# Start addresses of TensorE's operand tiles moved to multiples of 256 bytes

## The chip, the cores and the metric

The kernel runs on one core of a Trainium2 chip. The metric is device time in microseconds (us), from the start to the end of one execution; the median of 3 timed executions of the kernel before is 1410.64 us (1410.63 to 1410.92). TensorE does the matrix products, VectorE (DVE), ScalarE (ACT) and GpSimd (POOL) the elementwise work, and DMA queues move data between the device memory and SBUF, the on-chip memory of 128 partitions. A tile lies at the same byte address in each partition, and this case is about that address.

## The reference

Three layers follow each other. Everything is float32.

```python
# 1. retention: q, k, v of (8 batches, 8 heads, 576 positions, 64)
scores = q @ k.T / sqrt(64)
x = (scores * gamma[h] ** (i - j) where i >= j else 0) @ v     # -> 4608 tokens x 512
# 2. mixture of 8 experts, each token goes to one
logits = x @ w_gate + modality_bias[modality_id]
e = argmax(logits);  gate = softmax(logits)[e]
x = gate * (relu(x @ w1[e]) @ w2[e])                           # 512 -> 1024 -> 512
# 3. MLP
h = x @ w_in                                                   # 512 -> 2048
out = (h - tanh(h)) @ w_out                                    # 2048 -> 512
```

## The kernel before

**Stages.** The program runs three stages, one after the other, with a few steps of overlap. The attention stage goes through 36 tiles of 128 tokens in plain float32 (L309, L345, L353, L368) and routes the tokens (L409 to L461). The experts' stage goes through 12 units of 400 tokens of one expert, and the MLP stage through 9 blocks of 512 tokens.

**Matrix products.** In the last two stages each operand is split into a high and a low part of type float32r, so that a product takes three matmuls: high by high, high by low, low by high. A step (one of the 8 slices of 128 hidden features of an expert, or of the 16 of the MLP) has 12 matmuls for the first product (`blocks`, L657: 4 pieces `k` of the contraction by three) and 12 for the second (L859 to L861 in the experts' stage, L934 to L936 in the MLP stage). The second product of a step comes 2 (experts) or 3 (MLP) steps after the first.

**What streams and what is held.** In every first product (L657) the tokens stream: `xh[:, k]` and `xl[:, k]`, 400 columns of 4 bytes per partition in the experts' stage, and `yh[:, k]`, `yl[:, k]`, 512 columns, in the MLP stage; 128 x 128 pieces of weight are held. In the experts' second product `hi` and `lo` (400 columns) stream. In the MLP's second product the weights `wout` (512 columns) stream and pieces of `hi` and `lo` are held.

**Where tiles lie.** Memory comes from a stack of pools at each end of SBUF; a tile takes the address that the sizes of the tiles below it leave. Tiles of even units come from pool `xT_p[0]` and those of odd units from `xT_p[1]` (L136). The MLP's blocks alternate in the same way between `P["yT"]` and a pool `yTb` (L892). The scratch tiles `eh` and `el` of the MLP stage are cut from `xT_p[0]` (L896), which is free then.

**What sets the order.** Engines run their instructions in the order in which the code issues them (`manual_schedule`); a semaphore wait is added where a tile or its memory is reused. In the MLP stage `post3` gives ACT and DVE their work for a step, and `prep3` loads and splits the next block's tokens.

Of the kernel before, what the change touches and what calls it, by code (L numbers as in the profile page):

```python
# [8 lines left out]
F32 = mybir.dt.float32  # L9
F32R = mybir.dt.float32r  # L10
# [9 lines left out]
B, H, S, D = 8, 8, 576, 64  # L20
# [6 lines left out]
PERIOD = 9  # L27
# [4 lines left out]
NRG = NTILE // RG  # L32
UE = 400
SE = -(-UE // 128)
UMIN = -(-NT // UE)
UMAX = (NT - E) // UE + E
CAP = NT
# [2 lines left out]
UB = 512  # L40
# [3 lines left out]
KD = DM // 128  # L44
# [56 lines left out]
def kernel(tc, A, out):  # L101
    nc = tc.nc
    with ExitStack() as ctx:
# [14 lines left out]
        xT_p = [pool("xTa", 1), None]  # L118
        idt0 = keep.tile([128, SE], I32, name="idt0")
        pick = keep.tile([1, 2], I32, name="pick")  # L120
# [10 lines left out]
        xT, P = {}, {}  # L131

        def turn_rows(u, s, src, tp):

            if s == 0:
                p = xT_p[u != "t" and u % 2]  # L136
                xT[u] = (p.tile([128, KD, UE], F32R, name="xh"), p.tile([128, KD, UE], F32R, name="xl"))
            xh, xl = xT[u]
            w = min(128, UE - s * 128)
            c = slice(s * 128, s * 128 + w)  # L140
            tp = tp[:, :, 0:w]
            for k in range(KD):
                nc.tensor.transpose(tp[:, k], src[0:w, k * 128:(k + 1) * 128], ident[0:w, 0:w])
            nc.scalar.copy(out=xh[:, :, c], in_=tp)
            nc.vector.tensor_tensor(out=xl[:, :, c], in0=tp, in1=xh[:, :, c].bitcast(F32), op=ALU.subtract)  # L145

        def load_ids(base, idt):
            with nc.allow_non_contiguous_dma(reason="one id per partition and tile"):
                nc.sync.dma_start(out=idt, in_=slot_d[bass.ds(base, SE * 128), 0:1].rearrange("(s p) o -> p (s o)", p=128))

# [48 lines left out]
        with tc.manual_schedule():  # L199
            c1, c1r = ExitStack(), ExitStack()  # L200
            p1, p1r = pools(c1), pools(c1r)
            att = p1("att", 1)
# [10 lines left out]

            mask = att.tile([128, 2, TL], F32, name="mask")
            gx = att.tile([128, PERIOD, H // 2, TL], F32, name="gx")
            vsc = att.tile([128, PERIOD, H], F32, name="vsc")
            step = att.tile([128, PERIOD, H // 2], F32, name="step")
            state = [att.tile([128, H // 2, D], F32, name=f"state{i}") for i in range(2)]
            wg = const.tile([128, KD, 32], F32, name="wg")
            ltri = const.tile([128, 128], BF16, name="ltri")  # L220
            ones = const.tile([128, 128], BF16, name="ones")
# [296 lines left out]
            for t in range(NTILE):  # L518
                g, r = divmod(t, RG)
# [31 lines left out]
                if t == (EARLY + 1) * RG + 1:  # L551
# [3 lines left out]
                    load_ids(base, idt0)  # L555
                    x0 = [gld.tile([128, 2, DM], F32, name="vk") for _ in range(SE // 2)]
                    x0 = [x0[s // 2][:, s % 2] for s in range(SE)]
                    for s in range(SE):
                        gather_rows(s, idt0, x0[s], EARLY * RG * TL)
# [7 lines left out]
            def early(s):  # L567
                turn_rows(0, s, x0[s], ps_sc.tile([128, KD, TL], F32, name="sc") if s < 3 else ps_x.tile([128, 2, KD, TL], F32, name="xp")[:, 0])
# [63 lines left out]
            ls_last = route_a(g)  # L632
            for s in range(2, SE):
                early(s)
# [38 lines left out]
            yT = {}  # L673
# [5 lines left out]

            def split_y(b, yr, k, p):  # L680
                if k == 0:
                    yT[b] = (p.tile([128, KD, UB], F32R, name="yh"), p.tile([128, KD, UB], F32R, name="yl"))
                yh, yl = yT[b]
                nc.scalar.copy(out=yh[:, k], in_=yr[:, k])
                nc.gpsimd.tensor_tensor(out=yl[:, k], in0=yr[:, k], in1=yh[:, k].bitcast(F32), op=ALU.subtract)
# [7 lines left out]
            with ExitStack() as c2:  # L693
# [3 lines left out]
                ht_p = p2("ht2", 3)  # L697
# [3 lines left out]
                raws, raw_of, wsp, xg, regs, yos = {}, {}, {}, {}, {}, {}  # L701
                steps = [(u, f) for u in range(UMIN) for f in range(F1)]
                limits = {0: E * CAP, 1: E - 1, 2: NT, 3: 1}
# [47 lines left out]
                def post(i, hp, ht):  # L751
                    if hp is None:
                        split_w(i - 1, 1)
                        return
                    hi = ht_p.tile([128, UE], F32R, name="hi")
                    lo = ht_p.tile([128, UE], F32R, name="lo")
                    nc.scalar.activation(out=hi, in_=hp, func=ACTF.Relu)  # L757
                    nc.vector.scalar_tensor_tensor(out=lo, in0=hp, scalar=0.0, in1=hi.bitcast(F32), op0=ALU.max, op1=ALU.subtract)
                    ht[i] = (hi, lo)
                    if i > 0:  # L760
                        split_w(i - 1, 1)
                        load_raw(i - 1 + F1)
                        raws.pop(i - 1)
                    split_w(i + 2, 0)
                    if steps[i] in ((0, 0), (0, 1)):
                        for f in range(3 * i + 3, min(F1, 3 * i + 6)):
                            load_raw(f)
# [7 lines left out]
                yr0 = [None]  # L775
                idts = {}

                def swap():

                    c1r.close()  # L780
                    po, pr = pools(ctx), pools(c2)
                    P["yT"], P["yr"], P["wo"] = (po(n, 1, side="right") for n in ("yT", "yr", "wo"))
                    P["acc"] = po("acc", 4, space=PSUM, side="right")
                    P["id"] = pr("id2", 2, side="right")
                    P["yo"] = pr("yo2", 1, side="right")
                    cv2 = pr("cv2", 1, side="right")
                    cvs2.extend(conv(cv2, A["wo"][f], dst=wo_d[f]) for f in range(F3))
                    cvs2.extend(conv(cv2, A["wi"][f], winh[:, f], winl[:, f]) for f in range(F3))
                    for f in range(len(cvs2)):
                        fill2.extend(cvs2[f][1])  # L790
                        if f > 0:
                            fill2[-3] = lambda a=fill2[-3], b=cvs2[f - 1][2]: (a(), b())
                        if f + 2 < len(cvs2):
                            fill2[-1] = lambda a=fill2[-1], b=cvs2[f + 2][0]: (a(), b())
                    fill2.reverse()

                def prep(u, f):
                    if u == "t":
                        return
                    if u == 0 and f == 0:  # L800
                        rest_a()
                    if u == 0 and f == 1:
                        rest_b()
                    if u == 0 and f == 2:
                        rest_c()
                        swap()
                    d = 2 if u == 0 else 0
                    if u + 1 < UMIN:
                        if f == d:
                            idts[u + 1] = ids_of(u + 1)  # L810
                        if f == d + 1:
                            gather(u + 1, idts.pop(u + 1))
                        for s in {6: (0, 1), 7: (2, 3)}.get(f, ()) if u == 0 else range(f - F1 + SE + 1, f - F1 + SE + 2):
                            if 0 <= s < SE:
                                tr_x(u + 1, s)
                    while pend and cvs2:
                        load_raw(pend.pop(0))
                    if f == 3 and u - 1 in yos:
                        store(u - 1)
                        if (u - E + 1) * UE + E - 1 >= UB and yr0[0] is None:  # L820
                            yr0[0] = load_y(0)
                    if u == UMIN - 1 and f == 4:
                        load_wout(0, P["wo"])
                    if u == UMIN - 1 and f >= 4:
                        split_y(0, yr0[0], f - 4, P["yT"])
                    if u == 0 and f in (3, 4):
                        cvs2[f - 3][0]()
                    for _ in range(2 - f % 2 if u > 0 or f > 4 else 0):
                        if fill2:
                            fill2.pop()()  # L830

                def finish(u, acc):
# [6 lines left out]
                    yos[u] = yo  # L839
                    if u == "t" or u == UMIN - 1:  # L840
                        store(u)
# [32 lines left out]

                run_units(range(UMIN), None)
                while fill2:
# [10 lines left out]
            with ExitStack() as c3:  # L887
                p3 = pools(c3)
                wo_p = p3("wo3", 1)
                for f in range(1, F3):  # L890
                    load_wout(f, wo_p)
                yT2 = [P["yT"], p3("yTb", 1)]  # L892
                ht_p3 = p3("ht3", 4)
                o_p = p3("o", 1)
                vs = {}
                eh, el = (xT_p[0].tile([128, 3, UB], F32, name=n) for n in ("xh", "xl"))  # L896

                def post3(i, hp, ht):
                    old = vs.pop(i - 1, None)
# [89 lines left out]
```

## Time and profile before

| | us |
|---|---|
| median of the timed executions | 1410.64 |
| the profiled execution | 1411.06 |
| its span, first to last instruction | 1409.3 |
| attention stage, to the first matmul of the experts | 153 |
| experts' stage, to the first matmul of the MLP | 450 |
| MLP stage, to the end | 806 |

The stages overlap by a few steps; their borders are the starts of the first matmuls at L657, 152.99 and 603.40 us after the start. A row of the timeline or of the chain of waits begins with its start and its length, both in us, then the engine and the line; `x12` means that 12 instructions stand in the row. Matmuls are pipelined: the length of one row with one matmul says little, and the distance between the starts of two says what one costs.

### The profile page before, as it was taken

The page shows a single profiled execution, that of the slowest core. Times are in us where ns is not written, and L with a number is a line of the kernel's source. Part 1 is how long each engine was busy: PE and PEld are TensorE (multiplying, and loading weights), DVE is VectorE, ACT ScalarE, POOL GpSimd, SP SyncE. Part 2 cuts the span into 40 slices and gives each one's busy share as a digit, 9 for nine tenths or more (in the row PEclk, how much of TensorE's full clock was granted, in tenths as well). Part 3 has the DMA queues.
Part 4 walks back from the last instruction along what each step waited for, and adds up shares of the span by engine and source line. Part 5 has one row for each costly group of instructions (what it writes and reads, how often), then busy time and mean ns, then how long its engine had stood idle before and what let it go on. Part 6 is the DMA issues. An engine that isn't in the chain of part 4 may idle for free.

```text
span 1409.3 us, 22537 instructions
## 1 busy us (share of the span) xinstructions
PE 1386.3 (98%) x8427; PEld 1206.3 (86%) x8427; DVE 1045.1 (74%) x1762; ACT 692.8 (49%) x1302; POOL 218.2 (15%) x290
## 2 busy tenths in 40 slices
PE   8999999999999999999999999999999999999996
PEld 7888899999999999978888888888888888888884
DVE  5666778888888888568778777787777877778773
ACT  3323444444444444456555555555555555555542
POOL 4555311110000111101101111011110111101101
PEclk9999999999999999999999999999999999999998
DMA  9997644554844446261100001000010000100000
GB/s 372 405 337 261 206 137 130 123 127 142 229 92 92 92 122 169 67 248 32 40 22 30 30 1 42 19 30 30 1 45 16 30 30 0 46 16 1 30 0 30
DMA packets 65266, 136.50 MB, mean 97 GB/s; under 512 B 22656, under 2 KB 29376, under 8 KB 65152
## 3 DMA queue, kind: packets, MB, share of 16 engines
q1 hardware_dynamic: 50368, 96.77, 22.8%
q0 software_dynamic: 7296, 19.57, 4.1%
q10 hardware_dynamic: 7488, 18.67, 3.5%
q8 instruction: 68, 1.11, 0.3%
q14 instruction: 46, 0.38, 0.1%
HBM read 132.95 MB, written 39.80 MB: 123 GB/s over the span
## 4 chain that ended last, share of the span: by engine, by line
PE 51%; issue 5%; POOL 0%; POOLq 0%; ACT 0%
PE hp L657 26%; PE acc L935 8%; PE acc L934 8%; PE acc L936 8%; POOL out_dram L959 0%; POOLq L985 0%; POOL nopt L958 0%; ACT o L956 0%; POOLq L959 0%
## 5 line engine op out<-in xcount | busy, mean ns | idle before, releaser
L907 ACT ACTIVATE xh<-hp 128x512 f32<-128x512 f32 x144 | 86.1, 598 | 313.8 <-PE hp L657 292.1
L657 PE MATMUL hp<-yh,winh 128*128 128x512 f32 x576 | 226.6, 393 | 1.4 <-PEq L880 1.4
L657 PE MATMUL hp<-yl,winh 128*128 128x512 f32 x576 | 226.5, 393 | 0.0
L657 PE MATMUL hp<-yh,winl 128*128 128x512 f32 x576 | 226.4, 393 | 0.0
L935 PE MATMUL acc<-wout,hi 128*128 128x512 f32 x576 | 225.5, 391 | 0.0
L934 PE MATMUL acc<-wout,hi 128*128 128x512 f32 x576 | 225.3, 391 | 0.0
L936 PE MATMUL acc<-wout,lo 128*128 128x512 f32 x576 | 224.7, 390 | 0.0
L909 DVE TENSOR_TENSOR xl<-xh,hp 128x512 f32<-128x512 f32 x144 | 99.1, 688 | 161.2 <-ACT xh L908 161.2
L918 DVE SCALAR_TENSOR_TENSOR xl<-xh,xl 128x512 f32<-128x512 f32 x144 | 128.5, 893 | 15.4 <-DVE xl L917 0.5
L859 PE MATMUL acc<-hi,wh 128*128 128x400 f32 x384 | 137.1, 357 | 0.1
L657 PE MATMUL hp<-xl,wh 128*128 128x400 f32 x384 | 132.8, 346 | 0.5 <-DVE xl L145 0.5
L861 PE MATMUL acc<-hi,wl 128*128 128x400 f32 x384 | 132.7, 346 | 0.0
L657 PE MATMUL hp<-xh,wl 128*128 128x400 f32 x384 | 132.6, 345 | 0.2 <-DVE wl L733 0.2
L657 PE MATMUL hp<-xh,wh 128*128 128x400 f32 x384 | 132.1, 344 | 0.4 <-ACT wh L732 0.4
L860 PE MATMUL acc<-lo,wh 128*128 128x400 f32 x384 | 131.7, 343 | 0.0
L657 PEld LDWEIGHTS hp<-yh,winh 128*128 128x128 f32 x576 | 108.3, 188 | 25.7 <-PEq L880 1.7
L657 PEld LDWEIGHTS hp<-yh,winl 128*128 128x128 f32 x576 | 108.2, 188 | 24.6
L757 ACT ACTIVATE hi<-hp 128x400 fp32r<-128x400 f32 x96 | 48.4, 505 | 163.8 <-PE hp L657 163.8
L934 PEld LDWEIGHTS acc<-wout,hi 128*128 128x128 f32 x576 | 108.2, 188 | 24.2 <-ACT hi L912 0.3
L657 PEld LDWEIGHTS hp<-yl,winh 128*128 128x128 f32 x576 | 108.3, 188 | 23.9
L936 PEld LDWEIGHTS acc<-wout,lo 128*128 128x128 f32 x576 | 108.3, 188 | 23.6 <-DVE lo L913 0.4
L935 PEld LDWEIGHTS acc<-wout,hi 128*128 128x128 f32 x576 | 108.2, 188 | 23.1
(166 smaller groups left out, 2520.0 us busy)
## 6 DMA issues: line engine op xcount, KB each, us to landing
raw<-in_w_dram SPq DMA_DIRECT2D x91, 512.0 KB
qk<-in_qk_dram SPq DMA_DIRECT2D x36, 512.0 KB
vk<-in_vk_dram SPq DMA_DIRECT2D x36, 512.0 KB
y_d<-yo SPq DMA_DIRECT2D x12, 800.0 KB
yr<-y_d SPq DMA_DIRECT2D x9, 1024.0 KB
raw<-in_wo_dram SPq DMA_DIRECT2D x16, 512.0 KB
wo_d<-cv_em ACTq DMA_DIRECT2D x16, 512.0 KB
raw<-in_wi_dram SPq DMA_DIRECT2D x16, 512.0 KB
```

Source lines behind the costliest of these rows:

```text
L657: nc.tensor.matmul(out=hp, lhsT=lhs, rhs=rhs, start=j == 0, stop=j == 3 * KD - 1)
L757: nc.scalar.activation(out=hi, in_=hp, func=ACTF.Relu)
L859: nc.tensor.matmul(out=o, lhsT=wh[:, cs], rhs=hi, start=first, stop=False)
L860: nc.tensor.matmul(out=o, lhsT=wh[:, cs], rhs=lo, start=False, stop=False)
L861: nc.tensor.matmul(out=o, lhsT=wl[:, cs], rhs=hi, start=False, stop=last)
L907: nc.scalar.activation(out=u, in_=hp, func=ACTF.Square)
L909: nc.vector.tensor_tensor(out=v, in0=u, in1=hp, op=ALU.mult)
L918: nc.vector.scalar_tensor_tensor(out=v, in0=s, scalar=SQ_C, in1=v, op0=ALU.add, op1=ALU.mult)
L934: nc.tensor.matmul(out=acc[s], lhsT=hi, rhs=wh, start=first, stop=False)
L935: nc.tensor.matmul(out=acc[s], lhsT=hi, rhs=wl, start=False, stop=False)
L936: nc.tensor.matmul(out=acc[s], lhsT=lo, rhs=wh, start=False, stop=last)
```

## The change

Three things change. The attention stage's constants `vsc` and `step` move into one tile `small` behind `state`, padded to 512 bytes, so that `qk`, `vk`, `vs`, `a` and `state` begin at multiples of 256. The experts' streamed tiles get wider rows: 448 columns allocated for 400 used in `hi`, `lo` and in the odd units' `xh`, `xl`; 512 for 400 in the even units'. The MLP's even blocks take the even units' buffer instead of a pool of their own, a filler of 224 bytes stands ahead of `wout0`, and the scratch tiles, `o` and the MLP's `hi` and `lo` move to other memory. The leftover unit `"t"`, which these inputs don't reach, takes the odd units' buffer.

The start of each streamed or held operand, modulo 256 bytes, as the two programs were built (the matmuls counted are those of one execution):

```
operand                           matmuls      before                     after
qk, vk, vs, a, state (attention)  all of them  192 + 256 n, 192 + 512 n   0
xg (turned by TensorE)            held         128                        0
xh, xl, even units, k = 0 1 2 3   L657: 576    0 64 128 192               0
xh, xl, odd units,  k = 0 1 2 3   L657: 576    128 192 0 64               0
hi, lo of the experts (by turns)  L859-861     0 64 128, 192 0 64         0
weights of the experts            held         0                          0
yh, yl, even blocks (5 of 9)      L657: 960    224                        0
yh, yl, odd blocks (4 of 9)       L657: 768    0                          0
wout0 (one step in 16)            L934-936:108 224                        0
wout1 to wout15                   1620         0                          0
winh, winl, hi, lo of the MLP     held         0                          0
ident (streams through transposes)             128                        128
```

The 400 columns of the experts' stage are 1600 bytes, 512 columns are 2048, and 128 columns 512.

```diff
+LINE = 256
+UL = -(-UE * 4 // LINE) * LINE // 4
+PAD = 224
...
-                p = xT_p[u != "t" and u % 2]
-                xT[u] = (p.tile([128, KD, UE], F32R, name="xh"), p.tile([128, KD, UE], F32R, name="xl"))
+                p = xT_p[1 if u == "t" else u % 2]
+                xT[u] = [p.tile([128, KD, UB if p is xT_p[0] else UL], F32R, name=n)[:, :, 0:UE] for n in ("xh", "xl")]
...
-            vsc = att.tile([128, PERIOD, H], F32, name="vsc")
-            step = att.tile([128, PERIOD, H // 2], F32, name="step")
             state = [att.tile([128, H // 2, D], F32, name=f"state{i}") for i in range(2)]
+            small = att.tile([128, -(-PERIOD * H * 6 // LINE) * LINE // 4], F32, name="small")
+            vsc = small[:, 0:PERIOD * H].rearrange("p (r h) -> p r h", h=H)
+            step = small[:, PERIOD * H:PERIOD * H * 3 // 2].rearrange("p (r h) -> p r h", h=H // 2)
...
-                    yT[b] = (p.tile([128, KD, UB], F32R, name="yh"), p.tile([128, KD, UB], F32R, name="yl"))
+                    yT[b] = [p.tile([128, KD, UB], F32R, name=n) for n in ("xh", "xl")]
...
-                    hi = ht_p.tile([128, UE], F32R, name="hi")
-                    lo = ht_p.tile([128, UE], F32R, name="lo")
+                    hi, lo = (ht_p.tile([128, UL], F32R, name=n)[:, 0:UE] for n in ("hi", "lo"))
...
-                    P["yT"], P["yr"], P["wo"] = (po(n, 1, side="right") for n in ("yT", "yr", "wo"))
+                    po("line", 1, side="right").tile([128, PAD // 4], F32, name="line")
+                    P["yr"], P["wo"] = (po(n, 1, side="right") for n in ("yr", "wo"))
...
-                        split_y(0, yr0[0], f - 4, P["yT"])
+                        split_y(0, yr0[0], f - 4, xT_p[0])
...
-                yT2 = [P["yT"], p3("yTb", 1)]
-                ht_p3 = p3("ht3", 4)
-                o_p = p3("o", 1)
+                yT2 = [xT_p[0], p3("yTb", 1)]
+                o_p, e_p = (p3(n, 1, side="right") for n in ("o", "e3"))
+                ht_p3 = p3("ht3", 4, side="right")
                 vs = {}
-                eh, el = (xT_p[0].tile([128, 3, UB], F32, name=n) for n in ("xh", "xl"))
+                eh, el = (e_p.tile([128, 3, UB], F32, name=n) for n in ("eh", "el"))
```

No instruction is added, removed or moved on any engine. Some waits differ, because memory is reused by other tiles. SyncE's queue (SP), where the experts' stage loads the token list `idt` of unit 1 and behind it the next weights, before and then after:

```order
L482 DMA x_d<-xg 128x512 [waits DMAHW6_49,Activation_49]
L708 TENSOR_LOAD utab [waits DVE_49]
L149 DMA idt<-slot_d 128x4x1 [waits DMAHW7_49,DMASW7_49,DVE_49]
L708 TENSOR_LOAD utab
L725 DMA raw_2549<-in_w_dram 128x1024 [waits DMAHW0_49,DVE_49]
```

```order
L486 DMA x_d<-xg 128x512 [waits DMAHW6_49,Activation_49]
L712 TENSOR_LOAD utab [waits DVE_49]
L152 DMA idt<-slot_d 128x4x1 [waits DMASW7_49,DMAHW7_49,DVE_49,PE_49]
L712 TENSOR_LOAD utab
L729 DMA raw_2548<-in_w_dram 128x1024 [waits DMAHW0_49,DVE_49]
```

The load of `idt` waits for TensorE (PE) as well: its tile lies where the last group of attention output lay, which TensorE turns. ScalarE (ACT) at the start of the MLP stage, before and then after:

```order
L907 ACTIVATE xh<-hp 128x512 [waits DVE_49,PE_49,Activation_49]
L908 ACTIVATE xh<-hp 128x512
L915 ACTIVATE xh<-xh,epsb 128x512 [waits DVE_49,Activation_49]
L916 ACTIVATE xl<-xh,epsb 128x512 [waits DVE_49]
L907 ACTIVATE xh<-hp 128x512 [waits DVE_49,PE_49,Activation_49]
```

```order
L911 ACTIVATE eh<-hp 128x512 [waits DMAHW2_49,DMAHW0_49,PE_49]
L912 ACTIVATE eh<-hp 128x512
L919 ACTIVATE eh<-eh,epsb 128x512 [waits DVE_49,Activation_49]
L920 ACTIVATE el<-eh,epsb 128x512 [waits DVE_49]
L911 ACTIVATE eh<-hp 128x512 [waits DVE_49,PE_49,Activation_49]
```

The first write of the scratch tile waits for two DMAs, which saved converted weights (`wo_d`, L195) out of the memory that `eh` now takes, instead of for engines.

## Rows read from the trace of the kernel before

**Rows 1.** The page: TensorE's busy time, its granted clock in 40 slices.

```profile
PE 1386.3 (98%) x8427; PEld 1206.3 (86%) x8427; DVE 1045.1 (74%) x1762; ACT 692.8 (49%) x1302; POOL 218.2 (15%) x290
PEclk9999999999999999999999999999999999999998
```

**Rows 2.** What TensorE waited for: us in total, times, longest.

```profile
PE sc L309 <- DMA qk<-in_qk_dram: 6.1, 2, 4.7
PE hp L657 <- PEq L880: 1.4, 1, 1.4
PE hp L657 <- DVE xl L145: 0.5, 1, 0.5
```

**Rows 3.** Groups of matmuls of the last two stages: line, tiles, form, count, busy.

```profile
L657 PE MATMUL hp<-yh,winh 128*128 128x512 f32 x576 | 226.6, 393 | 1.4 <-PEq L880 1.4
...
L859 PE MATMUL acc<-hi,wh 128*128 128x400 f32 x384 | 137.1, 357 | 0.1
```

**Rows 4.** Stretches of MLP blocks 1 to 4: length, PE busy, clock, DMA.

```profile
684.03:771.18 87.15, 87.15 (x386) 1.00 0.07 25
771.18:859.98 88.80, 88.80 (x386) 1.00 0.07 24
859.98:947.12 87.14, 87.14 (x385) 1.00 0.07 25
947.12:1035.92 88.80, 88.80 (x385) 1.00 0.07 24
```

**Rows 5.** Chain of waits, MLP blocks 0 and 1: start, us, what.

```profile
603.40 11.44 PE hp L657 x48
...
628.73 2.80 PE hp L657 x12
...
634.27 2.80 PE hp L657 x12
...
700.51 2.72 PE hp L657 x12
...
706.03 2.75 PE hp L657 x12
...
711.50 2.72 PE hp L657 x12
716.94 2.72 PE hp L657 x12
```

**Rows 6.** Timeline of TensorE, unit 11: the first matmul of each piece k.

```profile
588.77 0.34 PE L657 MATMUL hp<-xh,wh 128*128 128x400 f32 x1
...
589.32 0.34 PE L657 MATMUL hp<-xh,wh 128*128 128x400 f32 x1
...
589.86 0.35 PE L657 MATMUL hp<-xh,wh 128*128 128x400 f32 x1
...
590.41 0.34 PE L657 MATMUL hp<-xh,wh 128*128 128x400 f32 x1
...
590.95 0.34 PE L859 MATMUL acc<-hi,wh 128*128 128x400 f32 x1
```

**Rows 7.** One stretch of the attention stage: length, PE, PEld, DVE, ACT, POOL, clock, DMA.

```profile
45.00:60.00 15.00, 15.00 (x256) 12.29 (x254) 9.89 (x27) 4.66 (x10) 10.40 (x14) 1.00 1.03 412
```

**Rows 8.** Timeline of TensorE in the attention stage.

```profile
65.37 0.63 PE L476 MATMUL m<-ident,xt 128*128 128x128 f32 x4
65.94 1.16 PE L309 MATMUL sc<-qk 64*128 64x128 f32 x16
```

**Rows 9.** Timeline of TensorE and SP's queue near the load of idt, ACT's later.

```profile
163.13 1.95 PE L476 MATMUL hp<-ident,xt 128*128 128x128 f32 x16
...
172.25 0.40 SPq L149 DMA_DIRECT2D idt<-slot_d  x1
...
606.53 0.60 ACT L907 ACTIVATE xh<-hp 128x512 f32<-128x512 f32 x1 [4.53 <-PE hp L657]
```

**Rows 10.** Instructions of L195: engine, count, ns min/median/max, first and last start.

```profile
L195 ACTq DMA_DIRECT2D wo_d<-cv_em x16: 326/326/338, 194.3 to 379.6; - x16
```

## The prediction

> **What bounds the kernel now.** I read the page first. [...] The last two stages hold six groups of 576 matmuls of 512 columns (the MLP) and six of 384 with 400 columns (the experts), one row of each shown in [rows 3]: 3456 and 2304 matmuls.
>
> Next I cut the MLP stage at its blocks. All blocks do the same work, with the same instructions, yet they alternate: odd blocks take 87.15 us, even ones 88.80 [rows 4]. The chain shows where: 12 matmuls at L657 take 2.72 us in an odd block and 2.80 in an even one, and a whole step, from one such row to the next, 716.94 - 711.50 = 5.44 us against 634.27 - 628.73 = 5.54 [rows 5]. No idle time lies between. By the table of start addresses the streamed tiles of even blocks begin 224 bytes past a multiple of 256, those of odd blocks at a multiple. That is the effect that the change acts on, in the trace already. The lengths of the blocks give the finer number: sixteen steps of 5.44 are 87.04, so an even block loses 88.80 - 87.04 = 1.76 us, about 0.107 per step and 9 ns per matmul at L657. Some 7 ns of that show within the 12 matmuls (80 ns by 12), the rest in the matmuls of the second product right behind.
>
> A second witness is `wout0`, the only streamed weight that begins at 224. Odd blocks have their tokens at 0, and in them just one step of 16 is longer, the one that streams `wout0`: 706.03 - 700.51 = 5.52, and the row after it 2.75 instead of 2.72 [rows 5]. Together that is the 0.11 us that an odd block has over 87.04.
>
> **The MLP stage, term by term.** After the change all 3456 streamed operands begin as in an odd block's ordinary step.
> - Blocks 2, 4, 6 and 8: 4 x 1.76 = 7.04 us. Block 8 is followed by the tail and can't be cut out in the same way; its 16 steps are taken as the others'.
> - Block 0: its first three steps have no second product, and these lose just the 80 ns of their own 12 matmuls; thirteen lose 0.107. With 0.05 for `wout0` (1.76 less 16 x 0.107) it is 0.24 + 1.39 + 0.05 = 1.68 us.
> - Blocks 1, 3, 5, 7 lose the 0.11 us of `wout0`: 0.44 us.
>
> Sum: 9.16 us. All of it lies on the path that sets the end. The next thing to be late would be `lo` for the first second product in block 0, since ACT begins only at 606.53 [rows 9]. TensorE arrives there four steps of 80 ns earlier; should all of that 0.3 us turn into a wait, the sum is 8.8.
>
> **The experts' stage.** Its starts move from 0, 64, 128 and 192 to 0. What is that worth? Unit 11 is odd, so its pieces k begin at 128, 192, 0 and 64. Their three matmuls each take 0.55, 0.54, 0.55 and 0.54 us [rows 6]: the aligned piece is no shorter. The mean is 2.18 us by 12, 182 ns. I take 0 for this stage. A count of the 256-byte lines that an operand touches says the same: 1600 bytes touch 7 lines from 0, 64, 128 or 192, while 2048 bytes touch 8 lines from 0 and 9 from 224. The lost time even scales so: 5.44 us by 24 is 227 ns with 8 lines and 9 ns more with 9, and 182 ns with 7 lines is 26 per line, as is (227 + 9) by 9. That would make the experts' matmuls bound by their 7 lines before and after. The bounds: if every one of the three quarters of operands that are off a multiple of 256 cost 9 ns, as in the even MLP blocks, 1728 x 9 = 15.6 us would go; if the aligned piece's equal time is all there is, nothing; and in the other direction the same 9 ns on 2304 matmuls would be a loss of 20.7. The rows on the very matmuls are nearest, hence 0.
>
> [...]
>
> **The attention stage.** Its operands go from 192 to 0. TensorE runs without a gap there while the DMA engines are full (share 1.03 [rows 7]), and float32 matmuls of 128 columns are slow for each byte that they stream: four transposes whose streamed tile begins at 128, before and after, are followed 0.57 us later, 142 ns each, and sixteen score matmuls take 1.16 us, two at a time on half the rows each [rows 8]. No row shows an aligned one. Bounds: 9 ns on each of the 36 x 8 pairs, and as much on the state and value products (four groups), is 36 x 8 x 4 x 9 ns = 10.4 us at most if nothing hides it, and the same on the other side if aligned starts collide; a faster load gains at most the 6.1 us of [rows 2]. I take 0, since the only rows on the matter, those of the experts' stage, show nothing for starts at multiples of 64, and 192 is one; the rows of the MLP concern 224, which isn't.
>
> **Waits that change.** The load of `idt` gets a wait for TensorE's last transposes of attention output. These end at 163.13 + 1.95 = 165.08, the load issues at 172.25 [rows 9]: 7 us of cover, and the weight loads queued behind it on SP don't move. The first write of `eh` waits for saves of `wo_d`, of which the last was issued at 379.6, against 606.53 for the write [rows 9, 10]. Both cost 0; without the cover the first would hold up the gather of unit 1, the second all of block 0.
>
> So the sum is -9.16 us: 1411.06 - 9.16 = 1401.9 for the profiled execution, which stands 0.4 above the median, and 1401.5 as a median.
>
> **Rivals.**
> 1. The experts gain too. An aligned matmul of 512 columns takes 227 ns; 112 columns fewer at 2.4 GHz are 46.7 ns less, 180. If what keeps the experts at 182 is an alignment debt that is carried from one matmul to the next, so that no single piece shows it (as the MLP's second product pays for the first), 2304 x 2.3 = 5.3 us go as well: 1396.2. For it: the debt is seen in [rows 5]. Against: a debt would not be spread so evenly over 0.55, 0.54, 0.55, 0.54.
> 2. Nothing comes of it: 1410.6. The even blocks' tiles and `wout0` share not only the 224 but also the upper end of SBUF, and if the place costs the time, not the start, the blocks would alternate no more but not gain as computed, or `wout0` would keep its step. For it: the two are not told apart by any row. [...] Against: odd blocks read `wout1` to `wout15` and tiles of their own over 70 KB of memory at one speed.
> 3. Slower: every streamed tile and every held weight of the experts now begins at the same place within 256 bytes, and TensorE reads both at once. If the two reads collide, at the 9 ns that the trace has for a disturbed read, 2304 x 9 = 20.7 us are lost against 9.2 gained: 1422. It turns the sign from 4 ns per matmul on. Against: an odd MLP block has both at 0 and is the fast one [rows 4], and so is the experts' piece k that begins at 0, whose weights do too [rows 6].
>
> **Chances.** Forecast 0.78, rival 1 0.14, rival 2 0.05, rival 3 0.03. A difference of 0.2% (2.8 us) can be told from no change here. Faster holds the first two, 0.92; same 0.05, slower 0.03. Range: down to rival 1 with a little from the attention stage, 1395.5; up to a loss of 1 ns on each matmul of the experts, 2.3 us, 1404.0.
>
> **What would show it.** In the trace after, all MLP blocks last 87.04 us, every row of 12 at L657 reads 2.72, and the step after `wout0` as well; the experts' pieces still take 0.54 or 0.55, and a step of the attention stage what it does now. If even blocks stay at 88.8, rival 2 holds; if the pieces drop to 0.53 or less, rival 1; if they rise, rival 3. A new gap on TensorE at 603 or near 180 us would mean that a wait is not covered.

## The result: 1398.2 us, and where the time went

The changed kernel takes 1398.17 us (median of 6 executions, 1397.69 to 1399.54), the kernel before 1411.05 in the same comparison: a ratio of 0.9908 (95% interval 0.9898 to 0.9919), so some 12.9 us less. The prediction said 1401.5, with 9.16 us less. Its profiled execution has a span of 1396.5 us against 1409.3.

TensorE is as full as in [rows 1], with less to do in the same 8427 records:

```profile
PE 1373.4 (98%) x8427; PEld 1201.6 (86%) x8427; DVE 1045.5 (75%) x1762; ACT 693.9 (50%) x1302; POOL 219.1 (16%) x290
```

It waits for little beside that, the largest entry 6.1 us in two times, for the first loads, as in [rows 2]. So the end is set by the distance between its matmuls.

Cut at the first matmul of the experts and at the first of the MLP, the two executions differ in two of three stages. The columns are start and end, length, then the busy time and count of PE, PEld, DVE, ACT and POOL, clock, DMA share and GB/s. Before:

```profile
0.00:153.00 153.00, 145.51 (x2454) 119.19 (x2454) 98.36 (x244) 50.24 (x117) 81.10 (x130) 1.00 0.90 332
153.00:603.40 450.40, 447.57 (x2518) 437.82 (x2519) 349.19 (x652) 197.18 (x400) 54.11 (x57) 1.00 0.49 130
603.40:1409.30 805.90, 793.23 (x3456) 649.33 (x3456) 597.58 (x868) 445.39 (x786) 82.96 (x104) 1.00 0.09 34
```

After:

```profile
0.00:153.00 153.00, 145.68 (x2454) 119.30 (x2454) 98.75 (x244) 50.21 (x116) 80.73 (x130) 1.00 0.90 331
153.00:599.70 446.70, 443.60 (x2518) 433.70 (x2519) 349.43 (x654) 197.49 (x400) 54.82 (x57) 1.00 0.49 131
599.70:1396.50 796.80, 784.12 (x3456) 648.63 (x3456) 597.31 (x867) 446.20 (x786) 83.52 (x104) 1.00 0.10 34
```

The attention stage is the same, the experts' stage lost 3.7 us, the MLP stage 9.1. The counts of TensorE's matmuls agree row by row, so the matmuls themselves got cheaper. The blocks of the MLP stage, which answer to [rows 4] (PE alone; block 0 and then 1 and 2):

```profile
599.73:678.69 78.96, 78.96 (x348) 1.00 0.41 138
678.69:765.73 87.04, 87.04 (x386) 1.00 0.07 25
765.73:852.77 87.04, 87.04 (x386) 1.00 0.07 25
```

Blocks 1 to 7 all last 87.04 us now. In the experts' stage the timeline of unit 11, one step as in [rows 6]:

```profile
589.42 0.34 PE L661 MATMUL hp<-xh,wh 128*128 128x400 f32 x1
589.60 0.34 PE L661 MATMUL hp<-xl,wh 128*128 128x400 f32 x1
589.78 0.34 PE L661 MATMUL hp<-xh,wl 128*128 128x400 f32 x1
...
591.58 0.34 PE L863 MATMUL acc<-hi,wh 128*128 128x400 f32 x1
```

The matmuls follow each other exactly 0.18 us apart, and twelve take 2.16 us; before they took 2.18, at distances of 0.17 to 0.19.

### The profile page after: what moved, and what is told of

Same layout as the page of the kernel before. It is cut to its first block, busy times and chain, and to the rows that moved or that the text cites. A ratio compares the mean times of both kernels' runs of the same rounds, so it can differ in the third digit from the quotient of the medians.

```text
span 1396.5 us, 22542 instructions
## 1 busy us (share of the span) xinstructions
PE 1373.4 (98%) x8427; PEld 1201.6 (86%) x8427; DVE 1045.5 (75%) x1762; ACT 693.9 (50%) x1302; POOL 219.1 (16%) x290
## 4 chain that ended last, share of the span: by engine, by line
PE 51%; issue 5%; POOL 0%; POOLq 0%; ACT 0%; DVE 0%
PE hp L661 26%; PE acc L940 8%; PE acc L938 8%; PE acc L939 8%; POOL out_dram L963 0%; POOLq L989 0%; POOL nopt L962 0%; ACT o L960 0%; POOLq L963 0%; DVE epsb L968 0%; DVE epsb L967 0%
## 5 line engine op out<-in xcount | busy, mean ns | idle before, releaser
L911 ACT ACTIVATE eh<-hp 128x512 f32<-128x512 f32 x144 | 86.4, 600 | 294.7 <-PE hp L661 274.2
L661 PE MATMUL hp<-xh,winh 128*128 128x512 f32 x576 | 224.1, 389 | 1.5 <-DVE epsb L968 1.5
L661 PE MATMUL hp<-xl,winh 128*128 128x512 f32 x576 | 224.1, 389 | 0.0
L661 PE MATMUL hp<-xh,winl 128*128 128x512 f32 x576 | 224.1, 389 | 0.0
L913 DVE TENSOR_TENSOR el<-eh,hp 128x512 f32<-128x512 f32 x144 | 99.1, 688 | 152.3 <-ACT eh L912 152.3
L922 DVE SCALAR_TENSOR_TENSOR el<-eh,el 128x512 f32<-128x512 f32 x144 | 128.6, 893 | 15.4 <-DVE el L921 0.5
L661 PEld LDWEIGHTS hp<-xh,winh 128*128 128x128 f32 x576 | 108.1, 188 | 24.2 <-PEq L884 1.8
L661 PEld LDWEIGHTS hp<-xl,winh 128*128 128x128 f32 x576 | 108.2, 188 | 22.4
L661 PEld LDWEIGHTS hp<-xh,winl 128*128 128x128 f32 x576 | 108.0, 188 | 22.4
```

Of the source, the lines that this page charges most:

```text
L661: nc.tensor.matmul(out=hp, lhsT=lhs, rhs=rhs, start=j == 0, stop=j == 3 * KD - 1)
L911: nc.scalar.activation(out=u, in_=hp, func=ACTF.Square)
L913: nc.vector.tensor_tensor(out=v, in0=u, in1=hp, op=ALU.mult)
L922: nc.vector.scalar_tensor_tensor(out=v, in0=s, scalar=SQ_C, in1=v, op0=ALU.add, op1=ALU.mult)
```

## The experiments

Theories at the start: A, a streamed operand pays for each line of 256 bytes that it touches (the prediction's count); B, each start has a price; C, only starts off a multiple of 64 do; D, the place in SBUF costs the time; E, the mixture of starts does. F came last: TensorE reads the operand that it streams and the weights that it will hold next at once (PE's 1373.4 us and PEld's 1201.6 lie in one span of 1396.5), and it is the distance between the two starts that counts. All kernels are the changed one with the edit shown, in which `...` marks what is left out; where starts vary by block or unit, that operand's tile has room for the shift and its view is shifted. (Where the MLP's tokens are shifted, the even units' tiles, which share their buffer, take the wider tile as well, with rows of 448 columns that still begin at 0; that edit is not shown.) Block times are those of steps 3 to 14 of a block, counted from 0: 12 steps, 288 matmuls, 65.28 us when a step takes 5.44. Kernels for which no time is given were executed once and are read by their blocks or units alone; the granted clock is 1.00 in all of these.

**One start for each MLP block.**

```diff
+STARTS = [0, 32, 64, 96, 128, 160, 192, 224, 16]
-                    yT[b] = [p.tile([128, KD, UB], F32R, name=n) for n in ("xh", "xl")]
+                    at = STARTS[b] // 4
+                    yT[b] = [p.tile([128, KD * UB + 64], F32R, name=n)[:, at:at + KD * UB].rearrange("p (k t) -> p k t", k=KD) for n in ("xh", "xl")]
```

> The changed kernel, with the streamed tokens of MLP blocks 0 to 8 beginning at 0, 32, 64, 96, 128, 160, 192, 224 and 16 bytes past a multiple of 256, in the buffers of the changed kernel. A step takes 5.44 us at 0. Theory A (each 256-byte line touched has a price: 8 lines from 0, 9 from any other start): 5.54 to 5.55 in all blocks from 1 to 8. Theory B (what counts is how far the start is into its line): a time that changes with the start, 5.55 at 224 (before showed 5.547), others anywhere between 5.44 and 5.7. Theory C (only starts off a multiple of 64 cost): 5.44 at 64, 128 and 192, 5.55 at 32, 96, 160, 224 and 16. Theory D (the place in SBUF cost the time, not the start): 5.44 in all blocks.

Blocks 0 to 8, each stretch 12 steps:

```profile
610.77:676.05 65.28, 65.28 (x289) 1.00 0.44 154
698.17:764.89 66.72, 66.72 (x289) 1.00 0.09 32
787.05:853.45 66.40, 66.40 (x289) 1.00 0.09 32
875.71:942.59 66.88, 66.88 (x290) 1.00 0.09 32
964.74:1031.06 66.32, 66.32 (x289) 1.00 0.09 32
1053.21:1119.69 66.48, 66.48 (x290) 1.00 0.09 32
1141.85:1208.33 66.48, 66.48 (x290) 1.00 0.09 32
1230.51:1297.07 66.56, 66.56 (x290) 1.00 0.04 16
1319.19:1385.51 66.32, 66.32 (x289) 1.00 0.04 17
```

Per step above 5.44: 120 ns at 32, 93 at 64, 133 at 96, 87 at 128, 100 at 160 and 192, 107 at 224 (as in the kernel before), 87 at 16. C falls (64, 128 and 192 cost), D falls (the five even blocks share one buffer and have four different times), A falls too: from all starts but 0 the same 9 lines are touched. B is left.

**More starts.** The same edit with 48, 4, 8, 80, 112, 144, 176, 208, 240.

> As the run with a start for each MLP block, with others: blocks 0 to 8 at 48, 4, 8, 80, 112, 144, 176, 208 and 240. All starts but 0 have cost 87 to 133 ns a step so far. Theory B: each of these costs something in that range. If small shifts are cheap, 4 and 8 lie near 0.

Of its nine blocks, those at 4, 8 and 240:

```profile
696.97:764.41 67.44, 67.44 (x289) 1.00 0.09 32
786.63:853.03 66.40, 66.40 (x289) 1.00 0.09 32
...
1318.00:1384.24 66.24, 66.24 (x289) 1.00 0.04 17
```

No shift is free. Four bytes cost the most, 180 ns a step or 15 ns per matmul; the least are 80 ns, at 80, 144 and 240.

**One start for each experts' unit**, weights held at 0 throughout.

```diff
+STARTS = [0, 0, 32, 64, 96, 128, 160, 192, 224, 16, 0, 0]
-                xT[u] = [...[:, :, 0:UE] for n in ("xh", "xl")]
+                at = STARTS[0 if u == "t" else u] // 4
+                xT[u] = [...[:, at:at + KD * UL].rearrange("p (k t) -> p k t", k=KD)[:, :, 0:UE] for n in ("xh", "xl")]
...
+                    at = STARTS[0 if steps[i][0] == "t" else steps[i][0]] // 4
-                    hi, lo = (ht_p.tile([128, UL], F32R, name=n)[:, 0:UE] for n in ("hi", "lo"))
+                    hi, lo = (ht_p.tile([128, UL + 64], F32R, name=n)[:, at:at + UE] for n in ("hi", "lo"))
```

> The changed kernel, with all streamed operands of one experts' unit (xh, xl, hi, lo) at one start: units 2 to 10 at 32, 64, 96, 128, 160, 192, 224, 16 and 0. A unit takes 36.73 us in the changed kernel and 36.98 to 37.12 before. Theory A (lines touched: 7 from 0 to 192, 8 from 224): 36.73 in all units but that of 224, which has 192 x 9 ns = 1.7 us more. Theory B (distance into the line): 36.73 at 0 alone, the others each with a time of their own, 37.0 to 37.1 as the mean over 64, 128, 192. Theory C (64 bytes): 36.73 at 0, 64, 128, 192 and up to 1.7 us more at 16, 32, 96, 160, 224. A fourth (E: it is the mixture of starts that costs, since each piece k and each tile of hi and lo began elsewhere): 36.73 in all units, as nothing is mixed within one.

Units 2 to 9 (starts 32 to 224, then 16):

```profile
228.51:265.25 36.74, 36.73 (x209) 1.00 0.51 131
265.25:301.97 36.72, 36.71 (x210) 1.00 0.54 131
301.97:339.09 37.12, 37.12 (x210) 1.00 0.43 130
339.09:376.31 37.22, 37.22 (x210) 1.00 0.76 214
376.31:413.41 37.10, 37.10 (x209) 1.00 0.51 130
413.41:450.61 37.20, 37.20 (x209) 1.00 0.40 88
450.61:487.90 37.29, 37.29 (x209) 1.00 0.45 87
487.90:524.92 37.02, 37.02 (x210) 1.00 0.45 117
```

With 400 columns 32 and 64 are free (36.73, as in units 2 to 10 of the changed kernel, which take 36.71 to 36.74), 96 to 224 cost 0.37 to 0.56 us a unit, 2 to 3 ns per matmul, and 16 costs 0.29. E falls: a unit without any mixture still pays. A falls again: 0 to 192 all touch 7 lines and differ, and 224 with 8 costs 0.56, not 1.7.

**More starts in the experts' stage:** 4, 8, 48, 80, 112, 144, 176, 208, 240 in units 2 to 10.

> As the run with one start for all streamed operands of a unit, with other starts: units 2 to 10 at 4, 8, 48, 80, 112, 144, 176, 208 and 240. There 400 columns cost 180 ns from 0, 32 and 64, 182 from 16 and 182.5 to 183.5 from 96 on. If a start off a multiple of 32 has a price of its own, about 182 at 4, 8 and 48 and 183 or more at the others; if only the place of the end counts (past the middle of the seventh line from 96 on), 180 at 4, 8, 48 and 183 from 80 on, where the 182 at 16 would not fit.

The first of them and the one at 208:

```profile
227.80:265.13 37.33, 37.32 (x210) 1.00 0.48 129
...
487.00:523.79 36.79, 36.79 (x209) 1.00 0.46 117
```

Neither reading fits: 4 bytes are again the dearest (37.33), and 208 is nearly free where 192 and 224 were not. The units at 48 and 112 are as near (36.80 and 36.85); single units at 0 read up to 36.86 in other executions, so these three can't be told from free.

**The experts' two halves at the old starts, and both.**

```diff
+                at = 0 if p is xT_p[0] else 32
+                xT[u] = [...[:, at:at + KD * UE].rearrange("p (k t) -> p k t", k=KD) for n in ("xh", "xl")]
```

> The changed kernel, with the rows of xh and xl back at 1600 bytes (starts 0, 64, 128, 192 by piece in even units, 128, 192, 0, 64 in odd ones); hi and lo stay at multiples of 256. Units took 37.05 before and 36.73 after, 0.32 apart. Theory B: the price of L657 alone, about half of it, 36.85 to 36.95, with matmuls of 182 at L657 and 180 at L859 to L861. Theory A: 36.73, and the whole gain of the experts' stage comes from elsewhere. Theory E: more than half, because the starts are mixed with those of hi and lo at every turn.

```diff
-                    hi, lo = (ht_p.tile([128, UL], F32R, name=n)[:, 0:UE] for n in ("hi", "lo"))
+                    hi, lo = (ht_p.tile([128, UL], F32R, name=n)[:, at:at + UE] for n, at in (("hi", 16 * (i % 3)), ("lo", 16 * (3, 0, 1)[i % 3])))
```

> The changed kernel, with hi at 0, 64, 128 and lo at 192, 0, 64 by turns as before; xh and xl stay at multiples of 256. Theory B: the other half, 36.85 to 36.95, and with the run before this one the parts add to 0.32. Theory A: 36.73. Theory E: more than half, the two parts together over 0.32.

> The changed kernel, with all streamed operands of the experts' stage at the starts of before (xh, xl by 64 per piece, hi and lo by turns); the MLP and attention stages stay changed. The gains of the two single parts, 0.185 us a unit for xh, xl and 0.18 for hi, lo, add: units of 37.05 us, 12 x 0.33 = 3.7 to 4.0 us slower than the changed kernel, 1402. If the parts share one debt, less than their sum.

One unit each, with the old `xh` and `xl`, with the old `hi` and `lo`, and with both:

```profile
265.86:302.79 36.93, 36.93 (x210) 1.00 0.54 131
```

```profile
265.20:302.10 36.90, 36.90 (x209) 1.00 0.54 131
```

```profile
303.76:340.81 37.05, 37.05 (x210) 1.00 0.41 131
```

Over units 2 to 10 the median is 36.91 us with either half and 37.05 with both, against 36.73: 0.18 for each half and 0.32 for both, so the halves add to within 0.04. The price lies in the product that has the old starts: there the starts of neighbouring matmuls are 182 ns apart (the median), in the other product 180, in both runs. With both halves the kernel takes 1402.15 us (1401.35 to 1402.61; ratio to before 0.9931, 0.9915 to 0.9948), 3.4 above the changed kernel's 1398.75 on the same chip.

**The MLP's old starts at the new places.**

```diff
+                at = 56 * (f == 0)
+                wout[f] = p.tile([128, 2 * DM + (64 if f == 0 else 0)], F32R, name=f"wout{f}")[:, at:at + 2 * DM].rearrange("p (a c) -> p a c", a=2)
...
+                    at = 56 * (b % 2 == 0)
+                    yT[b] = [p.tile([128, KD * UB + 64], F32R, name=n)[:, at:at + KD * UB].rearrange("p (k t) -> p k t", k=KD) for n in ("xh", "xl")]
```

> The changed kernel, with the streamed tokens of the even MLP blocks and wout0 at 224, in the changed kernel's places. The prediction's sum: even blocks at 88.80 us, odd ones at 87.15, 9.16 us slower than the changed kernel, 1407.3. If the place in SBUF had a part in it, less.

1407.65 us (1406.8 to 1410.15, ratio 0.9975, 0.9965 to 0.9984), 8.9 above the changed kernel. Blocks 1 and 2 have the times of [rows 4] to within a hundredth, at other addresses:

```profile
680.11:767.25 87.14, 87.14 (x385) 1.00 0.07 25
767.25:856.05 88.80, 88.80 (x385) 1.00 0.07 24
```

The old starts of the two stages account for 8.9 + 3.4 = 12.3 of the 12.7 us that separate the kernel before (1411.44) from the changed one on this chip.

**The identity, and the changed kernel again.** `ident`, the one streamed operand left at 128, gets a filler of 128 bytes ahead of it and another behind `nopt`.

```diff
+        keep.tile([128, 32], F32, name="fill0")
         ident = keep.tile([128, 128], F32, name="ident")
...
+        keep.tile([128, 32], F32, name="fill1")
```

> The changed kernel, with the identity (the streamed operand of all transposes, 128 columns of float32, the last one off a multiple of 256) moved from 128 to 0. If each streamed operand gains by it, 7 ns on some 350 transposes, 2.5 us at most, 1395.7. If float32 operands of 128 columns are too slow to be held up, as those of the attention stage (its units of time did not change from starts of 192 to 0), nothing: 1398.2.

> The changed kernel once more, on the chip of the other three, to compare them with: 1398.2.

1398.77 us against 1398.75: nothing of the 2.5 us shows, where single executions scatter by 1.

**Starts of held operands.** The MLP's `hi` and `lo`, of which TensorE holds 128 columns, vary by block; all streams stay at 0.

```diff
+                        at = STARTS[(i - 1) // F3] // 4
+                        hi, lo = (ht_p3.tile([128, UB + 64], F32R, name=n)[:, at:at + UB] for n in ("hi", "lo"))
```

> The changed kernel, with the tiles that TensorE takes weights from in the MLP's second product (hi, lo) at 0, 32, 64, 96, 128, 160, 192, 224 and 16 in blocks 0 to 8; what streams stays at 0. If held operands have a price like streamed ones (128 columns are 512 bytes: 2 lines from 0, 3 from elsewhere), 12 matmuls a step by about 7 ns, steps of 5.52. If weight loads are hidden behind the matmul ahead of them (188 ns within 227), 5.44 in all blocks, and the change needed only the streamed operands.

Blocks 5 (start 160), 6 (192) and 8 (16), where block 0 (start 0) takes 65.28:

```profile
1049.79:1116.58 66.79, 66.79 (x289) 1.00 0.09 32
1138.85:1204.49 65.64, 65.64 (x290) 1.00 0.09 33
...
1314.67:1379.95 65.28, 65.28 (x289) 1.00 0.04 17
```

Held operands have prices too, 30 to 126 ns a step (0 at 16), though they are loaded while the matmul ahead of them streams. That is where theory F came from. The timeline of block 1 (start 32), where the first product ends and the load (LDWEIGHTS) of the first piece of `hi` begins:

```profile
708.70 0.40 PE L662 MATMUL hp<-xh,winl 128*128 128x512 f32 x1
708.71 0.19 PEld L939 LDWEIGHTS acc<-wout,hi 128*128 128x128 f32 x1
708.94 0.39 PE L939 MATMUL acc<-wout,hi 128*128 128x512 f32 x1
```

In the mean over the block's 12 steps the 2nd to 11th matmul of the first product take 227 ns each and the 12th, during which `hi` is loaded, 235, though its own two operands begin at 0. So what is read meanwhile slows it, as F has it.

**Everything at 160.** All operands that the MLP streams or holds begin at 160, but for the tokens, which vary by block.

```diff
+STARTS = [160, 0, 32, 64, 96, 128, 160, 192, 224]
+            wres.tile([128, 40], F32, name="fill0")
             winh = wres.tile([128, F3, DM], F32R, name="winh")
             winl = wres.tile([128, F3, DM], F32R, name="winl")
+            wres.tile([128, 24], F32, name="fill1")
...
+                wo_p.tile([128, 40], F32, name="fill2")
                 for f in range(1, F3):
                     load_wout(f, wo_p)
+                wo_p.tile([128, 24], F32, name="fill3")
...
+                p3("fill", 1, side="right").tile([128, 24], F32, name="fill4")
                 ht_p3 = p3("ht3", 4, side="right")
```

(`wout0` and the tokens are shifted as in the runs above.)

> The changed kernel, with everything that the MLP's matmuls stream or hold at 160 past a multiple of 256 (winh, winl, wout, hi, lo), and the streamed tokens of blocks 0 to 8 at 160, 0, 32, 64, 96, 128, 160, 192, 224. So in block 6 (and 0) all operands begin at the same 160. Streaming from 160 beside held weights at 0 cost 100 ns a step, holding at 160 beside streams at 0 127 ns. Theory F (the distance between the two reads counts: TensorE reads both at once): 5.44 in block 6, and 5.53 to 5.57 in block 1 and the others. Theory B (each start has its own price, whatever the other's): 5.44 + 0.10 + 0.13 and as much again for wout and the held hi and lo, 5.7 to 5.9 in block 6, less in block 1, where the streamed tokens lie at 0.

Blocks 0 to 8:

```profile
616.00:681.28 65.28, 65.28 (x290) 1.00 0.44 154
703.44:770.32 66.88, 66.88 (x290) 1.00 0.09 32
792.47:858.79 66.32, 66.32 (x289) 1.00 0.09 32
880.94:947.42 66.48, 66.48 (x290) 1.00 0.09 32
969.58:1036.06 66.48, 66.48 (x290) 1.00 0.09 32
1058.24:1124.80 66.56, 66.56 (x290) 1.00 0.09 32
1146.66:1211.94 65.28, 65.28 (x289) 1.00 0.09 33
1234.06:1300.78 66.72, 66.72 (x289) 1.00 0.04 16
1322.94:1389.34 66.40, 66.40 (x289) 1.00 0.04 17
```

Blocks 0 and 6, where all begin at 160, have the full speed of the changed kernel: 65.28. Block 1, whose tokens lie at 0, a multiple of 256, is the slowest. And all the times are those of the first experiment at the same distance, to the hundredth: tokens at 192 (32 past the weights) 66.72, at 224 (64 past) 66.40, at 0 (96 past, counted round 256) 66.88, then 66.32, 66.48, 66.48 and 66.56 for 128, 160, 192 and 224. B falls and F holds in what it says of distances: a start has no price of its own, only its place relative to the other operands has. That the other operand is the held `winh` and `winl`, and not `wout`, `hi` or `lo`, which moved with them, follows from where the price falls: 80 of the 107 ns that a step loses at 224 lie within the 12 matmuls of the first product [rows 5], which, up to the load at their end, read no others. Why two reads at unequal starts disturb each other no run shows.

## Why the prediction was right, and where it was not

- **The MLP stage, right to 0.1 us.** The sum was 9.16 us, the stage lost 9.1; block 0 was to lose 1.68 and went from 80.63 to 78.96. The trace of before held both states side by side, and the sum was made of whole blocks. Putting the old starts back cost 8.9 us.
- **Its reason was wrong.** The even blocks were not slow because they touched 9 lines; they were slow because their tokens lay 224 bytes from `winh` and `winl` modulo 256 (66.56 us for 12 steps at that distance, with the weights at 0 and at 160, against 65.28). The two readings give the same time for this change, as it brings all to 0, so the number says nothing for the lines. The lines didn't even fit the prediction's own rows: 182 by 7 and 236 by 9 are 26 ns per line, but 227 by 8 is 28.
- **The experts' stage is the step that failed.** "The rows on the very matmuls are nearest, hence 0" should have been 3.7 us, 1.6 ns on each of 2304 matmuls. The four pieces at 0.55, 0.54, 0.55 and 0.54 us could not show it: rows in hundredths are 10 ns apart, and three matmuls differ by 5. A longer count was at hand: twelve matmuls in 2.18 us, 182 ns each, against rival 1's 180, which the changed kernel reaches exactly. The lines (7 from each start, so nothing to gain) then supported a wrong 0.
- **Rival 1** had the right side and 1396.2 for 1398.2. Its 46.7 ns for 112 columns, 2.4 columns per ns, is what the changed kernel shows: 226.7 ns for a matmul of 512 columns and 180.0 for one of 400. Its 2.3 ns doesn't follow from the rows: 2.18 us by 12 is 181.67 ns, 1.67 above 180, and 2304 by 1.67 are 3.8 us, close to the 3.7 that went. Nor could its sign have come: pieces of "0.53 or less" would be under three matmuls at its own 180 ns, 0.54, which the forecast allowed as well. Its reason, a debt carried from one matmul to the next, stays open: in even MLP blocks 27 of a step's 107 ns came after the 12 matmuls that have the start, but in the experts' stage a single half at its old starts slowed mainly its own product.
- **Rival 2** fell: the old starts at new places gave the old times, and one buffer gave four.
- **Rival 3** had two reads disturbing each other, which the run on held operands bears out, but the wrong way round: they are undisturbed when both begin at the same place (12 steps take 65.28 us with all at 0 and with all at 160).
- **The attention stage, right at 0, by luck.** It took 152.97 us to the first matmul of the experts, against 152.99. The prediction took its 0 from that of the experts, which was wrong. All of its operands lay at 192 before, streams and weights alike, so F, if it holds for float32, gives 0 as well. Whether float32 matmuls would feel a distance at all was tried only with the identity, which didn't move the time (1398.77 us against 1398.75).
- **The waits, right at 0.** TensorE's longest wait at the start of the MLP stage was 1.4 us before [rows 2] and is 1.5 after, and near 180 us none is over 0.5 us, before or after.

## What to carry to other kernels

Where float32r matmuls follow each other without a gap, give what is streamed and what is held the same start modulo 256 bytes: here a streamed operand that began elsewhere than the held one cost 6.7 to 15 ns on each matmul of 512 columns, and 0 to 3 ns on each of 400. Which start made no difference here (12 steps took 65.28 us at 0 and at 160), so the cheapest filler may be the one that shifts the fewer tiles. Look for it in a trace as groups with the same instruction at two speeds that depend on the buffer alone, as in the blocks of [rows 4]. Before reading a small price as 0, multiply it by the count and compare it with the grain of the rows: here 1.6 ns by 2304 was 3.7 us, and rows of 10 ns hid it.

## What the runs showed of the hardware

- Where streamed operand and held weights shared their start modulo 256, a float32r matmul of 512 columns took 226.7 ns (5.44 us by 24) and one of 400 columns 180.0 (2.16 by 12). The 112 columns between them are 46.7 ns, 2.4 columns per ns; if all columns take that, 13.3 ns of either matmul are left over, an estimate from these two widths alone.
- Shifting the streamed tokens to any of 17 other starts cost 80 to 180 ns per 12 matmuls of 512 columns, 4 bytes the most. Shifting the held `hi` and `lo` cost 30 to 126, and at 16 nothing.
- What stays open: why the price jumps between neighbouring distances; why 400 columns have free distances (32, 64) and streams of 512 have none; and why shifting the held operand by 16 costs nothing while streams at 240, the same distance, cost 80 ns. So equal starts gave full speed wherever they were tried, but the price of unequal ones was only listed, not explained.
